# Two chained feed-forward layers: products in two 64-row halves of TensorE, two chunks at once

## The chip, the core and the metric

The kernel runs on one core of one Trainium2 chip. The metric is the device time of one execution in microseconds. Three runs of the kernel before took 1233.02, 1232.05 and 1232.23 us; the median is 1232.23.

## What is computed

Input is x (2 x 4096 tokens of 192 numbers, float32) and weight_gen (8 heads x 7 taps per token). A short causal convolution with per-token softmax weights comes first, then two feed-forward layers without bias, 192 to 2048 to 192:

```
w = softmax(weight_gen, axis=-1)
attn[b, s, h, :] = sum over k of w[b, s, h, k] * x_padded[b, s + k, h, :]
h = attn @ w_in;   g = h * cos(h);            y = g @ w_out      # layer 0
h = y @ moe2_w_in; g = maximum(0.01 * h, h);  out = g @ moe2_w_out   # layer 1
```

Everything is float32. The kernel keeps that precision by splitting each operand into a high and a low part of a shorter float type (fp32r) and adding the products hi x hi, lo x hi and hi x lo.

## The kernel before

**Tiles.** The 8192 tokens are 16 blocks of 512. A block's x stands transposed: 128 of its 192 numbers on the partitions of tiles hi and lo, the remaining 64 on both halves of the partitions of rh and rl (`x_tiles`, L388). The 2048 hidden units are 16 chunks of 128 (NF), so there are 2 layers x 16 blocks x 16 chunks = 512 chunks.

**One chunk** (`chunk`, L698). `hidden` (L708) forms h for 128 hidden units and 512 tokens in one bank of PSUM with five matmuls of 128 rows and 512 columns; the last two take the 64 remaining rows with their high weights on one half of the partitions and their low weights on the other:

```
terms = [(ihi, hi), (ilo, hi), (ihi, lo), (ir, rh), (ir, rl)]
for i, (w, v) in enumerate(terms):
    nc.tensor.matmul(h(), w[:, c], v(), start=i == 0, stop=i == len(terms) - 1)
```

Then comes the activation. In layer 0 (L743 to L753): ScalarE (or VectorE) rounds h / 2 pi to whole turns (L724), VectorE takes the angle (L731), ScalarE the sine (L736), VectorE multiplies by h (L741), ScalarE copies the high part (L262, a helper's line) and GpSimd subtracts to get the low part (L267). In layer 1 (L755 to L758): ScalarE's leaky ReLU, a copy of the high part, and VectorE's subtraction. `project_hi` (L767) and `project_lo` (L772) add the chunk's share of the second product with five more matmuls into two accumulators of the block, am (128 outputs) and ar (the other 64, high and low weights on different output partitions).

**Blocks.** `attention` (L395) makes a block's convolution on VectorE by token rows, and TensorE transposes it with six matmuls of 128 columns in two pieces (`turn`, `turn_rest`, L483 and L484); the first two blocks sum their seven taps on TensorE itself (`attention_summed`, L487, with L510). `turned` and `place` (L522, L543) split into high and low; ScalarE and VectorE copy the 64 remaining rows to the other half of the partitions (L552, L553). At a block's end `take` (L807) reads the accumulators; after layer 0 it makes the x tiles of layer 1, after layer 1 TensorE transposes back (L846, L847) and SyncE's queue stores (L853).

**Weights.** `weights` (L559) decodes 64-bit weights into high and low parts for 8 groups (2 layers x 4) of four chunks, in the first 200 us or so. ScalarE, VectorE and GpSimd share the work; four small DMAs a group (L666) move the remaining rows of w_in to their half of the partitions.

**Order.** Two streams of (layer, block) go side by side (L270 to L273), in the middle one with layer 0 and one with layer 1; the loop at L287 takes a chunk from each in turn (seq). Each operation is put into a plan with a due place in that order, a cost for each engine that may do it, and its buffers (`Plan.op`, L66); `Plan.emit` (L89) then goes through its own clock and issues, engine by engine, what can start first, near ties by due place. Each engine runs what it got strictly in that order. PSUM's eight banks are split: four shared by h and transposes, four accumulators (L242, L243). Rings hold 5 tiles g, 4 hi and 4 lo (L704 to L706). At the start TensorE is kept running by transposes of a constant (`keep_going`, L861).

## Time and profile before

| | |
|---|---|
| runs | 1233.02, 1232.05, 1232.23 us |
| span of the profiled execution, first to last instruction | 1230.4 us |
| granted TensorE clock, mean | 0.997 |
| TensorE busy (matmuls) | 1212.0 us, 98% |
| TensorE busy (weight loads, beside matmuls) | 998.8 us, 81% |
| VectorE, ScalarE, GpSimd busy | 891.2, 848.6, 449.1 us |
| DMA moved | 39.51 MB, mean 32 GB/s |

The profiled execution's own time is not listed beside its span; the median of the runs is 1.8 us above the span. Engines in rows: PE is TensorE's matmuls, PEld its weight loads, DVE is VectorE, ACT ScalarE, POOL GpSimd, SP SyncE; a small q behind a name means the engine's queue issuing DMAs. In a row, "out<-in" names tiles, "128x512" is partitions by elements, "x256" a count; after a bar come busy microseconds in all and mean nanoseconds of one, and then idle time ahead of it with what ended that. Matmuls are pipelined, so their lengths overlap: the distance from start to start is what one costs in a dense stretch.

### The profile page before, as it was taken

Reading aid. Unit: us, or ns where it says so; the run is one execution under the profiler, and the core shown is the slowest. Engines: PE = TensorE matmul, PEld = TensorE weight load, DVE = VectorE, ACT = ScalarE, POOL = GpSimd, SP = SyncE. Lnnn points to the kernel's source line nnn. Section 1 sums busy time; section 2 is a strip of 40 time slices with the busy share of each in tenths; the row PEclk is TensorE's granted clock in tenths of the full one; section 3 lists DMA queues with packets and bytes.
Section 4 is the critical chain, followed back from the end, with each engine's and each line's share of the span. In section 5 each row is a group of like instructions: output and inputs, shape, how many; then the busy total and the mean of one; then the engine's idle time right before and its main releaser. Section 6 shows DMA issues by size and latency. Waiting matters only on the chain.

```text
span 1230.4 us, 15323 instructions
## 1 busy us (share of the span) xinstructions
PE 1212.0 (98%) x5464; PEld 998.8 (81%) x5464; DVE 891.2 (72%) x1359; ACT 848.6 (69%) x1545; POOL 449.1 (36%) x340
## 2 busy tenths in 40 slices
PE   7999999999999999999999999999999999999998
PEld 6787877888888888888888888888888888888886
DVE  7988898988776777668577776767768586655433
ACT  5899767787766777676576767757666676655654
POOL 4878724663332423323232332323323333322000
PEclk9999999999999999999999999999999999999999
DMA  7344210200001010100101001010100100000000
GB/s 206 98 125 127 84 46 1 78 1 1 1 18 43 1 46 1 46 1 1 46 1 60 1 10 36 1 45 1 46 1 1 46 1 14 1 1 14 1 14 26
DMA packets 15469, 39.51 MB, mean 32 GB/s; under 512 B 1828, under 2 KB 8482, under 8 KB 15392
## 3 DMA queue, kind: packets, MB, share of 16 engines
q1 hardware_dynamic: 15392, 38.53, 9.8%
q8 instruction: 43, 0.70, 0.2%
q14 instruction: 34, 0.28, 0.1%
HBM read 30.13 MB, written 6.29 MB: 30 GB/s over the span
## 4 chain that ended last, share of the span: by engine, by line
PE 91%; DVE 4%; ACT 2%; DMA 1%; issue 1%; POOL 0%; SPq 0%; POOLq 0%; DVEq 0%; ACTq 0%
PE h L712 44%; PE acc0m L768 5%; PE acc1r L770 4%; PE acc0m L769 4%; PE acc0r L770 4%; PE acc0r L773 4%; PE acc1m L774 4%; PE acc1r L773 4%; PE acc0m L774 4%; PE acc1m L768 4%; PE acc1m L769 4%; DMA w00out<-in_moe_w_out 1%; DVE pr L436 1%; PE pm L839 1%; PE tm L476 0%
## 5 line engine op out<-in xcount | busy, mean ns | idle before, releaser
L267 POOL TENSOR_TENSOR lo<-g,hi 128x512 fp32r<-128x512 f32 x240 | 338.1, 1410 | 606.5 <-ACT hi L262 517.1
L731 DVE SCALAR_TENSOR_TENSOR g<-g,h 128x512 f32<-128x512 int32 x256 | 174.8, 685 | 158.7 <-ACT g L724 158.0
L267 DVE TENSOR_TENSOR lo<-h,hi 128x512 fp32r<-128x512 f32 x272 | 186.5, 688 | 93.5 <-ACT hi L262 91.8
L724 ACT ACTIVATE g<-h 128x512 int32<-128x512 f32 x233 | 138.3, 595 | 133.5 <-PE h L712 132.3
L755 ACT ACTIVATE h<-h 128x512 f32<-128x512 f32 x256 | 148.9, 582 | 86.5 <-PE h L712 85.6
L736 ACT ACTIVATE g<-g 128x512 f32<-128x512 f32 x256 | 160.3, 629 | 57.0 <-DVE g L731 56.2
L741 DVE TENSOR_TENSOR g<-h,g 128x512 f32<-128x512 f32 x240 | 164.6, 687 | 35.5 <-ACT g L736 30.5
L262 ACT ACTIVATE hi<-g 128x512 fp32r<-128x512 f32 x238 | 149.3, 629 | 47.1 <-DVE g L741 45.8
L262 ACT ACTIVATE hi<-h 128x512 fp32r<-128x512 f32 x228 | 135.3, 594 | 9.8 <-DVE h L741 1.2
L768 PE MATMUL acc0m<-hi,ohi 128*128 128x512 f32 x256 | 101.9, 398 | 2.4 <-ACT hi L262 2.4
L712 PE MATMUL h<-x0hi,ihi 128*128 128x512 f32 x256 | 100.3, 392 | 1.9 <-DVE lo L267 0.8
L773 PE MATMUL acc0r<-lo,or 128*128 128x512 f32 x256 | 100.6, 393 | 1.3 <-POOL lo L267 1.2
L768 PE MATMUL acc1m<-hi,ohi 128*128 128x512 f32 x256 | 101.8, 398 | 0.0
L712 PE MATMUL h<-x1hi,ihi 128*128 128x512 f32 x256 | 100.9, 394 | 0.4 <-DVE lo L267 0.4
L770 PE MATMUL acc1r<-hi,or 128*128 128x512 f32 x256 | 99.9, 390 | 0.4 <-POOL or L267 0.4
L769 PE MATMUL acc0m<-hi,olo 128*128 128x512 f32 x256 | 100.0, 391 | 0.0
L770 PE MATMUL acc0r<-hi,or 128*128 128x512 f32 x256 | 100.0, 391 | 0.0
L774 PE MATMUL acc0m<-lo,ohi 128*128 128x512 f32 x256 | 99.8, 390 | 0.0
L769 PE MATMUL acc1m<-hi,olo 128*128 128x512 f32 x256 | 99.8, 390 | 0.0
L773 PE MATMUL acc1r<-lo,or 128*128 128x512 f32 x256 | 99.8, 390 | 0.0
L712 PE MATMUL h<-x1rh,r 128*128 128x512 f32 x256 | 99.8, 390 | 0.0
L712 PE MATMUL h<-x1lo,ihi 128*128 128x512 f32 x256 | 99.8, 390 | 0.0
(254 smaller groups left out, 2462.6 us busy)
## 6 DMA issues: line engine op xcount, KB each, us to landing
xt<-in_x SPq DMA_DIRECT2D x12, 960.0 KB, 5.0
out<-osb SPq DMA_DIRECT2D x16, 384.0 KB, 2.6
smw<-in_weight_gen SPq DMA_DIRECT2D x3, 448.0 KB
xt<-in_x SPq DMA_DIRECT2D x3, 384.0 KB, 6.9
xt<-in_x SPq DMA_DIRECT2D x2, 576.0 KB, 7.5
r<-whi SPq DMA_DIRECT2D x16, 64.0 KB, 2.0
r<-wlo SPq DMA_DIRECT2D x16, 64.0 KB, 2.0
w00out<-in_moe_w_out SPq DMA_DIRECT2D x2, 384.0 KB, 8.4
```

The costliest lines, as they stand in the source:

```text
L262: nc.scalar.activation(out=out, in_=in_, func=AF.Copy)
L267: eng[e].tensor_tensor(out=out, in0=a, in1=b.bitcast(F32), op=ALU.subtract)
L712: nc.tensor.matmul(h(), w[:, c], v(), start=i == 0, stop=i == len(terms) - 1)
L731: nc.vector.scalar_tensor_tensor(out=g(), in0=g().bitcast(I32), scalar=-2 * math.pi, in1=h(), op0=ALU.mult, op1=ALU.add)
L736: nc.scalar.activation(out=g(), in_=g(), func=AF.Sin, bias=math.pi / 2)
L741: nc.vector.tensor_tensor(out=h() if bank_low else g(), in0=h(), in1=g(), op=ALU.mult)
L755: op(pos + 0.6, {"ACT": 0.58}, lambda e: nc.scalar.activation(out=h(), in_=h(), func=AF.Prelu, alpha=0.01), [kh], [kg], [h])
L768: nc.tensor.matmul(am(), ohi[:, f % GF, :], ghi(), start=first, stop=False)
L769: nc.tensor.matmul(am(), olo[:, f % GF, :], ghi(), start=False, stop=False)
L770: nc.tensor.matmul(ar(), orr[:, f % GF, :], ghi(), start=first, stop=False)
L773: nc.tensor.matmul(ar(), orr[:, f % GF, :], glo(), start=False, stop=last)
L774: nc.tensor.matmul(am(), ohi[:, f % GF, :], glo(), start=False, stop=last)
```

## The change

- TensorE is used as two halves of 64 rows. A chunk of even number has its first product on the lower half of the partitions (0 to 63), one of odd number on the upper half; so two chunks of the same block go at once. The 192 rows are three parts of 64, with three kinds of product each: 9 half-products. In the second product, each half takes 64 of a chunk's 128 hidden units: 5 half-products a chunk on each side. A pair of chunks so has 19 steps on either side.
- For that, x lies in three tiles of high and low parts: xn, xs (xn with its partition halves exchanged, written by two DMAs, `crossed`) and xr (the remaining 64 rows on both halves, the second by DMA where copies by ScalarE and VectorE stood). Loads of w_in put the chunks' rows straight on their half; the whi and wlo tiles and their DMAs go.
- The order of steps is a list for each side, made ahead: one side forms h of pair p and then adds pair p - 2 to the accumulators, the other adds pair p - 3 and then forms h of p. Where a side is about to write an accumulator's bank that the other side wrote, a wait (a nop on TensorE's queue with a semaphore) is put in front, on a matmul at least four steps back (APART). The list is cut into pieces that the plan issues in order; all pieces have one order key.
- The streams: after the first two blocks, whole blocks follow one another, layer 0 and layer 1 in turn.
- All eight banks of PSUM are one pool, with at most six for h. g, hi and lo have four tiles each at first; once all weights are decoded, the space of the raw weights becomes four more of each.
- The six transposes of a block are issued together, at a planner's cost that has 0.43 us more. Preparing a block is due eight chunk places ahead, not two.

The core of the diff:

```diff
--- before.py
+++ after.py
-    GAP = 3
-    TURN = 8
+    TURN = 12
     STAGGER = 6
+    LAG = 2
+    APART = 4
+    SWITCH = 0.43
+    FEW = 4
+    HELD = 6
+    EASE = 8
+    SIDES = (slice(0, P // 2), slice(P // 2, P))
...
-    xts = ctx.enter_context(tc.tile_pool(name="xts", bufs=4))
+    xts = ctx.enter_context(tc.tile_pool(name="xts", bufs=3))
     work = ctx.enter_context(tc.tile_pool(name="work", bufs=1))
-    ps = ctx.enter_context(tc.tile_pool(name="ps", bufs=4, space=PSUM))
-    psa = ctx.enter_context(tc.tile_pool(name="psa", bufs=1, space=PSUM))
+    raws = tc.tile_pool(name="raws", bufs=1, side="right")
+    space, places = {"raws": raws.__enter__()}, {}
+    ps = ctx.enter_context(tc.tile_pool(name="ps", bufs=1, space=PSUM))
...
+    def kept(tag, line):
+
+        def make():
+            (_, i) = b.held[0]
+            if (tag, i) not in places:
+                pool = work if i < FEW else space["late"]
+                places[tag, i] = pool.tile([P, T], F32 if tag == "g" else F32R, tag=f"{tag}{i}", bufs=1, name=f"{tag}{i}")
+            return places[tag, i]
+
+        b = Buf(make, tag, FEW, line=line)
+        return b
+
...
     def bank(name, kind):
-        return Buf(lambda: ps.tile([P, T], F32, tag="ps", name=name), "ps", 4, [kind])
+
+        def make():
+            (_, i) = b.held[0]
+            if ("ps", i) not in places:
+                places["ps", i] = ps.tile([P, T], F32, tag=f"ps{i}", name=f"ps{i}")
+            return places["ps", i]
+
+        b = Buf(make, "ps", 8, [kind] if kind else [])
+        return b
...
+    late = [(0, 2), (0, 3)]
+    for b in range(2, NB - 2):
+        late += [(1, b), (0, b + 2)]
+    streams = [[(0, 0), (1, 0), *late, (1, NB - 2), (1, NB - 1)], [(0, 1), (1, 1)]]
...
+    OUT = [(j, i) for j in range(2) for i in range(3)] + [(j, i) for j in range(2) for i in (3, 4)]
+    PAIRS = len(seq) // 2
+    lists = [[], []]
+    for p in range(PAIRS + LAG + 1):
+        for side in range(2):
+            q = p - LAG - side
+            ins = [("in", p, i) for i in range(9)] if p < PAIRS else []
+            outs = [("out", q, i) for i in range(10)] if 0 <= q < PAIRS else []
+            lists[side] += outs + ins if side else ins + outs
+
+    def part(step):
+        kind, p, i = step
+        return (kind, p) if kind == "in" else (kind, p, i // 3 if i < 6 else 2)
+
+    def bank_of(step):
+        kind, p, i = step
+        return (*seq[2 * p][1:3], "r" if i > 5 else "m") if kind == "out" else None
+
+    steps, at, last, known, log = [], [0, 0], {}, -1, []
+    while at[0] < len(lists[0]) or at[1] < len(lists[1]):
+        now = [None, None]
+        for side in range(2):
+            if at[side] == len(lists[side]):
+                continue
+            step = kind, p, i = lists[side][at[side]]
+            if side and kind == "out" and i == 0 and at[0] < len(lists[0]) and lists[0].index(("out", p, 9)) >= at[0]:
+                continue
+            before = last.get((1 - side, bank_of(step))) if kind == "out" else None
+            wait = None
+            if before is not None and before[1] > known:
+                if before[0] > len(steps) - APART:
+                    continue
+                wait = max(n for t, n in log if t <= len(steps) - APART)
+                known = wait
+            log.append((len(steps), len(log)))
+            if kind == "out":
+                last[side, bank_of(step)] = log[-1]
+            now[side] = (step, wait)
+            at[side] += 1
+        steps.append(now)
...
+    def crossed(m, b, due):
+        xn, xs, xr = x_of[m, b]
+        for j in range(2):
+            to, of_ = SIDES[j], SIDES[1 - j]
+            op(due, {"SP": 0.8}, lambda e, to=to, of_=of_: nc.sync.dma_start(
+                out=xs()[to].bitcast(F32), in_=xn()[of_].bitcast(F32)), [("xhi", m, b), ("xlo", m, b)], [("xs", m, b, j)], [xn, xs])
...
-        op(last, {"PE": 0.44}, turn, [("xam", b, q) for q in kinds] + ["ident"], [("tm", b)], [xa, tm])
-        op(last + 0.1, {"PE": 0.22}, turn_rest, [("xbr", b, q) for q in kinds] + ["ident"], [("tr", b)], [xb, tr])
+        def both(e):
+            turn(e)
+            turn_rest(e)
+
+        op(last, {"PE": 0.66 + SWITCH}, both, [(k, b, q) for q in kinds for k in ("xam", "xbr")] + ["ident"],
+           [("tm", b), ("tr", b)], [xa, xb, tm, tr])
...
-            op(due, {"ACT": 0.39}, lambda e, p=p, c=c: copy(e, rh()[p, c], v()[p]), [key], [("rh", m, b, i)], [rh, src])
-            op(due + 0.2, {"DVE": 0.42 if m == 0 else (0.41,)}, lambda e, p=p, c=c: minus(e, rl()[p, c], v()[p], rh()[p, c]),
-               [key, ("rh", m, b, i)], [("rl", m, b, i)], [rh, rl, src])
-        for i, ((p, c), (p2, _)) in enumerate(zip(halves, reversed(halves))):
-            op(due + 0.4, {"ACT": 0.39}, lambda e, p=p, p2=p2, c=c: copy(e, rh()[p2, c], v()[p]), [key], [("rh", m, b, 2 + i)], [rh, src])
-            op(due + 0.6, {"DVE": (0.29,)}, lambda e, p=p, p2=p2, c=c: copy(e, rl()[p2, c], rl()[p, c].bitcast(F32)),
-               [("rl", m, b, i)], [("rl", m, b, 2 + i)], [rl])
+            op(due, {"ACT": 0.39}, lambda e, p=p, c=c: copy(e, xr()[p, 0, c], v()[p]), [key], [("rh", m, b, i)], [xr, src])
+            op(due + 0.2, {"DVE": 0.42 if m == 0 else (0.41,)}, lambda e, p=p, c=c: minus(e, xr()[p, 1, c], v()[p], xr()[p, 0, c]),
+               [key, ("rh", m, b, i)], [("rl", m, b, i)], [xr, src])
+            op(due + 0.5, {"SP": 0.4}, lambda e, p=p, p2=SIDES[1 - i], c=c: nc.sync.dma_start(
+                out=xr()[p2, :, c].bitcast(F32), in_=xr()[p, :, c].bitcast(F32)), [("rh", m, b, i), ("rl", m, b, i)], [("rx", m, b, i)], [xr])
...
-        h = bank(f"h{m}_{b}_{f}", ("hq", 3))
-        g = temp([P, T], "g", 5, f"g_{pos}", line=f"g{st}")
-        ghi = temp([P, T], "hi", 4, f"hi_{pos}", F32R, f"hi{st}")
-        glo = temp([P, T], "lo", 4, f"lo_{pos}", F32R, f"lo{st}")
-
-        def hidden(e):
-            c = slice((f % GF) * P, (f % GF + 1) * P)
-            terms = [(ihi, hi), (ilo, hi), (ihi, lo), (ir, rh), (ir, rl)]
-            for i, (w, v) in enumerate(terms):
-                nc.tensor.matmul(h(), w[:, c], v(), start=i == 0, stop=i == len(terms) - 1)
-
-        reads = [((n, "a"), "hi", 0), ((n, "a"), "lo", 0)]
-        reads += [((n, "r"), i, j) for i in ("hi", "lo") for j in range(2)]
-        reads += [("xhi", m, b), ("xlo", m, b)] + [(i, m, b, j) for i in ("rh", "rl") for j in range(4)]
+        h = bank(f"h{m}_{b}_{f}", ("hq", HELD))
+        g, ghi, glo = (kept(i, f"{i}{st}") for i in ("g", "hi", "lo"))
+        side = f % 2
+        rows, j = SIDES[side], f % GF // 2
+
+        def hidden(i):
+            x, d = [(xn, side), (xr, 2), (xs, 1 - side)][i // 3]
+            w, v = [(ihi, 0), (ilo, 0), (ihi, 1)][i % 3]
+            return nc.tensor.matmul(h(), w[rows, j, d], x()[rows, v], start=i == 0, stop=i == 8)
+
+        first, last = f < 2, f >= NF - 2
+        if f == 0:
+            acc_of[st] = [bank(f"acc{m}{i}_{b}", None) for i in "mr"]
+        am, ar = acc_of[st]
+
+        def project(to_side, i):
+            to, w, v = [(am, ohi, ghi), (am, olo, ghi), (am, ohi, glo), (ar, orr, ghi), (ar, orr, glo)][i]
+            r = SIDES[to_side]
+            return nc.tensor.matmul(
+                to(), w[r, f % GF, :], v()[r], start=f == 0 and to_side == 0 and i in (0, 3),
+                stop=f == NF - 1 and to_side == 1 and i in (2, 4),
+            )
...
+        def run(e):
+            for now in nows:
+                for side, x in enumerate(now):
+                    if not x:
+                        continue
+                    (kind, p, i), wait = x
+                    if wait is not None:
+                        q = nc.tensor.nop()
+                        tc.add_manual_dep(q.ins, ran[wait].ins.name, sync, reason="bank")
+                    if kind == "in":
+                        ran.append(made["in", 2 * p + side][0](i))
+                    else:
+                        ran.append(made["out", 2 * p + OUT[i][0]][0](side, OUT[i][1]))
+
+        op(due, {"PE": len(nows) * MM}, run, reads, writes, bufs)
```

## Rows read from the trace of the kernel before

**Rows 1.** The page: busy times, and the chain by engine and by line
```profile
PE 1212.0 (98%) x5464; PEld 998.8 (81%) x5464; DVE 891.2 (72%) x1359; ACT 848.6 (69%) x1545; POOL 449.1 (36%) x340
PE 91%; DVE 4%; ACT 2%; DMA 1%; issue 1%; POOL 0%; SPq 0%; POOLq 0%; DVEq 0%; ACTq 0%
```

**Rows 2.** Table by stage: start:end, length, busy us (instructions) of each engine
```profile
core 0: us, PE busy (x) PEld busy (x) DVE busy (x) ACT busy (x) POOL busy (x), PEclk, DMA share, GB/s
0.00:20.00 20.00, 15.43 (x102) 14.15 (x103) 13.96 (x24) 8.66 (x17) 7.91 (x16) 0.91 0.79 221
20.00:200.00 180.00, 171.36 (x771) 137.85 (x770) 162.41 (x232) 146.22 (x255) 114.68 (x92) 0.99 0.31 93
...
400.00:500.00 100.00, 100.00 (x448) 82.71 (x448) 76.43 (x117) 72.72 (x132) 34.55 (x24) 1.00 0.04 15
...
1215.00:1230.40 15.40, 10.67 (x52) 8.25 (x50) 4.17 (x7) 6.09 (x12) 0.00 (x0) 1.00 0.14 53
```

**Rows 3.** Timeline of TensorE, 399.8 to 411.6 us: start, length, engine, line, operation
```profile
399.81 0.39 PE L712 MATMUL h<-x0hi,ilo 128*128 128x512 f32 x1
399.81 0.19 PEld L712 LDWEIGHTS h<-x0lo,ihi 128*128 128x128 f32 x1
...
400.04 0.39 PE L712 MATMUL h<-x0lo,ihi 128*128 128x512 f32 x1
400.04 0.19 PEld L712 LDWEIGHTS h<-x0rh,r 128*128 128x128 f32 x1
...
411.60 0.39 PE L768 MATMUL acc1m<-hi,ohi 128*128 128x512 f32 x1
```

**Rows 4.** Groups by line: one of the twenty alike; busy us, mean ns
```profile
L712 PE MATMUL h<-x1rl,r 128*128 128x512 f32 x256 | 99.7, 390 | 0.0
```

**Rows 5.** Timeline of TensorE around transposes (groups of four and two)
```profile
8.43 0.60 PE L510 MATMUL tr<-ident,pr 128*64 128x128 f32 x4
...
10.62 0.60 PE L510 MATMUL tm<-ident,pr 128*128 128x128 f32 x4
...
1221.46 0.60 PE L839 MATMUL pm<-ident,om 128*128 128x128 f32 x4
...
1221.90 0.38 PE L843 MATMUL pr<-ident,s 128*128 128x128 f32 x2
...
1222.35 0.39 PE L769 MATMUL acc1m<-hi,olo 128*128 128x512 f32 x1
```

**Rows 6.** Timeline of TensorE around one early stall
```profile
52.74 0.40 PE L774 MATMUL acc0m<-lo,ohi 128*128 128x512 f32 x1
54.28 0.51 PE L768 MATMUL acc0m<-hi,ohi 128*128 128x512 f32 x1 [1.15 <-ACT hi L262]
54.62 0.40 PE L769 MATMUL acc0m<-hi,olo 128*128 128x512 f32 x1
```

**Rows 7.** Stage 60 to 92 us: its table, and its layer-0 angles by line
```profile
60.00:92.00 32.00, 32.00 (x143) 26.47 (x142) 28.68 (x46) 29.09 (x51) 23.89 (x21) 1.00 0.40 120
...
L731 DVE SCALAR_TENSOR_TENSOR g<-g,h 128x512 f32<-128x512 int32 x14 | 9.6, 682 | 2.2 <-ACT g L724 2.0
```

**Rows 8.** Groups by line: ScalarE's three passes of a layer-0 chunk
```profile
L736 ACT ACTIVATE g<-g 128x512 f32<-128x512 f32 x256 | 160.3, 629 | 57.0 <-DVE g L731 56.2
L262 ACT ACTIVATE hi<-g 128x512 fp32r<-128x512 f32 x238 | 149.3, 629 | 47.1 <-DVE g L741 45.8
...
L724 ACT ACTIVATE g<-h 128x512 int32<-128x512 f32 x233 | 138.3, 595 | 133.5 <-PE h L712 132.3
```

**Rows 9.** DMA issues (KB each, median us to landing), and TensorE's first hidden product
```profile
out<-osb SPq DMA_DIRECT2D x16, 384.0 KB, 2.6
...
r<-whi SPq DMA_DIRECT2D x16, 64.0 KB, 2.0
...
20.58 0.47 PE L712 MATMUL h<-x0hi,ihi 128*128 128x512 f32 x1
```

More of the change, by code (lines that the diff above doesn't have):

```diff
@@ L169, in emit @@
                 self.at = max(self.at, o.due)
+            for b in o.bufs:
+                b.end = max(b.end, o.end)
             o.fn(e)
@@ L606, in weights @@
                 k = n, i, pn
[L607 removed]
+                due = need[m, g * GF] + WDUE[i]
                 def size(e, raw=raw, t=t, c=c):
@@ new lines, in conv_attention_moe_moe, with more @@
+    gate = Buf(lambda: None, "raw", 3, [("raw", 3)] * 2 + [("wa", 2)] * 2)
+    def more(e):
+        raws.__exit__(None, None, None)
+        space["late"] = ctx.enter_context(tc.tile_pool(name="late", bufs=1, side="right", reuse_waits="tile"))
+        for tag in ("g", "hi", "lo"):
+            plan.slots[tag] += [(gate.end, FEW + i) for i in range(FEW)]
+    weighed = [k for k in plan.writers if isinstance(k, tuple) and len(k) == 3 and k[1] in ("hi", "lo")]
+    op(0, {"SP": 0.0}, more, weighed, ["late"], [gate])
@@ new lines, in conv_attention_moe_moe @@
+    built = 0
+    for key, nows in pieces:
+        dues = []
+        for side, at in enumerate(key):
+            if at:
+                dues.append(2 * at[1] + side + (0 if at[0] == "in" else 2 * LAG + 1 + 0.3 * at[2]))
+                while at[0] == "in" and built <= 2 * at[1] + 1:
+                    st, m, b, f = seq[built]
+                    if f == 0 and m == 0:
+                        attention(b, tops[b])
+                    chunk(built, *seq[built])
+                    built += 1
+        piece(key, nows, max(dues))
```

266 lines of the change are left out of this document (134 added, 132 removed).

## The prediction

> **What bounds the kernel now.** I read the page's busy times and its chain first. TensorE is busy 98% of the span and holds 91% of the chain of work that ended last [rows 1]: nearly all of the time is matmuls one behind another. The table by stage then shows where that isn't so [rows 2]: the first 20 us (TensorE busy 15.4), the 180 us after them (171.4, while VectorE is busy 162.4, or 90%), and the last 15.4 us (10.7). In a stage from the middle TensorE is never idle, VectorE is busy 76%, ScalarE 73% and GpSimd 35%.
>
> So the price of one matmul decides. In the timeline a matmul of 512 columns starts at 399.81 us and the 52nd after it at 411.60 [rows 3]: 11.79 / 52 = 0.2267 us from start to start, though each lasts 0.39, so neighbours overlap by 0.163. Its weight load of 0.19 us begins as the matmul ahead of it starts; nothing waits for loads. There are twenty groups of 256 such matmuls [rows 4], so 5120 x 0.2267 = 1160.7 us. The other 344 of TensorE's 5464 are transposes [rows 1]; twenty of them take 10.62 - 8.43 = 2.19 us [rows 5], 0.109 each, 37.6 in all. That leaves 1230.4 - 1160.7 - 37.6 = 32.1 us of start, early waits and tail. The runs' median, 1232.23, is 1.8 above the span, and I carry that over unchanged. A difference of 0.2%, 2.5 us, is about the least that can be told from none.
>
> **The change, part by part.** *Halves of 64 rows.* A chunk's hidden product takes 9 half-products (three 64-row parts of the 192 rows, times hi x hi, lo x hi, hi x lo) where 5 full ones, ten halves, ran before; the lo x lo product of the last 64 rows goes. The second product stays at 10 halves. Each half of TensorE thus has 9 + 10 = 19 matmuls per two chunks, against 20 full ones. Going through the list that the diff builds gives 4889 steps (256 x 19 = 4864, and 25 for the lag at both ends; 50 steps have one half idle). The trace has no two half matmuls side by side. Its bounds are far apart: 0.2267 us a step if the halves run together, 0.4533 if one after the other. I take 0.2267, because each half then sees in a step just what the array sees now, one load of 128 columns and 512 columns of data, and the paths that both halves share bear it by the nearest row: a load and a transpose together pass in 0.109 us [rows 5], two such pairs in 0.219, under 0.2267. Term: (4889 - 5120) x 0.2267 = **-52.4 us**.
>
> *The sequencer.* A step issues four instructions. Two per 0.109 us is a rate that was reached, so 19,456 loads and matmuls, 688 for transposes and 924 new waits take at most 21,068 x 0.0547 = 1152 us, against 1108.3 + 37.6 = 1146 of array time: from 0 to +6; I take 0, since that row is a bound and need not be the sequencer's own pace.
>
> *Changes between whole and half array.* Transposes still use 128 rows. Today a group of six between matmuls costs only itself: from its start at 1221.46 to the second matmul after it at 1222.35 there are 0.89 us [rows 5], and 6 x 0.109 + 0.2267 is 0.88. By that row the term is 0. The Trainium skill (TensorEngine Tiling, section Tiling Modes, Key Properties) says that a change of tiling mode, not merely of tile, drains TensorE; no run here shows it yet. A drain is priced by rows: the overlap of 0.163 is lost at each of the two changes, 0.33 a group, and if the next load can't start before it either, 0.188 more at each, 0.70. Thirty groups (14 of inputs, 16 of outputs, each now issued as one piece) and about seven meetings with the second block's summed transposes give 0 to 26; in the middle of the drained prices, 37 x 0.5 = **+18.5 us**. By the first row alone the forecast would be 18.5 lower.
>
> *Waits between the halves.* The list puts a wait into TensorE's queue 924 times, so that one half's writes to an accumulator's bank are done before the other half's begin. All later matmuls stand behind it. It waits for a matmul at least four steps back, 0.91 us earlier, that is done after 0.39 [rows 3]; 0.52 us are left, more than a load's 0.188. Below, 0; above, a queue run dry at each wait: after a stall the first two matmuls are 0.34 us apart (54.28 to 54.62 [rows 6]), 0.113 more than usual, 104 us in all. I take **0**, by the 0.52 us of cover.
>
> *Crossed copies by DMA.* Each block's x is written into the other 64 partitions by SyncE's queue: two DMAs of 256 KB, and one or two of the remainder. The ScalarE and VectorE copies that did the latter go, as do 32 weight DMAs. SyncE issues in order, so a crossed copy can stand behind an output store that waits for its tile. A 64 KB copy lands after 2.0 us, a 384 KB store after 2.6 [rows 9]; preparation is eight chunk places, some 17 us, ahead, so in the middle they cost 0. Without that cover a block would wait some 2.5 us. At the start there is none: first matmul at 20.58 us [rows 9], crossed x needed from its seventh step, so +2.0 - 1.4 = about **+1 us** (0 to 3).
>
> *Start-up.* From 20 to 200 us VectorE is at 90% and TensorE already waits. If VectorE can't be driven harder, the 4.5% are not gained there: 180 x 0.045 = 8.1 us; otherwise 0. The hi and lo tiles number four until the weights are done, and a pair now waits two pairs for its second product. I take **+6 us**, near the upper end.
>
> *Layers one at a time.* A layer-0 chunk needs three ScalarE passes [rows 8], 1.85 us; alone that is 3.71 of a pair's 19 x 0.2267 = 4.31 us (86%), plus block work. From 60 to 92 us today's kernel runs layer 0 only: 14 chunks, TensorE 32.0 of 32, ScalarE 91% and VectorE 90% busy [rows 7]. So 0; what the wait costs without this is a rival. PSUM's one pool: two accumulators and some three h banks of eight stay under the cap: 0.
>
> *Tail.* Its one-sided steps are in the 4889.
>
> Sum: -52.4 + 18.5 + 1 + 6 = -26.9, from 1232.2 to **1205 us**.
>
> **Rivals.** *Layer 0 bound by ScalarE* (chance 0.10). For: 86% and block work at once, where layers were mixed before. Against: rows 7. A wait of 0.15 us in each of 128 layer-0 pairs gives 19 us: 1224.
>
> *The 924 waits are paid* (0.13). If the sequencer doesn't run ahead of the array, a wait restarts it: at half of rows 6's 0.113 us, 52 us, so 1258, slower than before. It decides from 26.9 / 924 = 0.029 us a wait. For: issue has only 0.008 us of room per step by the bound above. Against: the 0.52 us of cover. The Trainium skill (TensorEngine Tiling, Gotcha 1: PSUM Pressure) says that row tiles can't be at one PSUM bank together, so the waits can't simply go; no run here shows that.
>
> *The halves overlap only in part* (0.11, "it doesn't do what it says"). It decides from 26.9 / 4889 = 0.0055 us, a step of 0.2322; at 0.240 it is 1205 + 65 = 1270, with no overlap at all over 2290. For: no row has two matmuls side by side. Against: two load pairs in 0.219. The Trainium skill (TensorE: Matmul & The Clock Gate, Part 3, Measured speedup vs the span model) has 3.07x for four row tiles; at that share of the ideal a step would be 0.295, an estimate, and the time 1539. No row here bears that out.
>
> **How the numbers follow.** The forecast has 0.66; its own range runs from 1180 (only the steps) to 1217 (drains at 0.70, start 3, start-up 8.1). Layer 0 reaches 1224, the waits reach 1258; 1180 to 1262 leaves out some 0.05 below and 0.12 above. Faster: 0.66, 0.07 of the layer-0 case and 0.02 of mild waits, 0.75. Same: 0.04, from the edges of those two. Slower: 0.10 of the waits and 0.11 of the overlap, 0.21.
>
> **What would show it.** Half matmuls of two partition halves at the same start, pairs 0.2267 us apart: right; 0.232 or more: wrong. A gap of 0.3 to 0.7 us in matmul starts around each transpose group: drains. Gaps at the bank waits, every fifth step or so, would show that rival; matmuls waiting for GpSimd or ScalarE in layer-0 blocks the other. Start-up: the two-hundredth microsecond reached with no more chunks than before. The forecast fails if the middle isn't 4 to 4.5% faster.

## The result, and the profile after

The changed kernel takes **1209.68 us** (median of 4 runs, 1209.06 to 1211.85) against 1232.37 for the kernel before, measured beside it: a ratio of 0.9817, 95% interval 0.9804 to 0.9831. That is 22.7 us or 1.8% less, where 27 less were forecast. Its profiled execution spans 1208.1 us, against 1230.4 before. In a few executions the granted clock was lower and the time much longer (1470.97 us at 0.75 in one of them); the times below leave these out, and two kernels whose profile fell in one are told by their times alone.

The page: busy times, the chain by engine, and three of its DMA issues (KB each, median us to landing).

```profile
PE 1182.8 (98%) x10072; PEld 1016.0 (84%) x10072; DVE 886.1 (73%) x1299; ACT 847.0 (70%) x1484; POOL 443.0 (37%) x331
...
PE 92%; DMA 2%; DVE 2%; POOL 1%; issue 1%; ACT 1%; SPq 0%; DVEq 0%; POOLq 0%; ACTq 0%
...
x0s<-x0n SPq DMA_DIRECT2D x32, 256.0 KB, 3.8
x1s<-x1n SPq DMA_DIRECT2D x32, 256.0 KB, 3.7
out<-osb SPq DMA_DIRECT2D x16, 384.0 KB, 2.8
```

TensorE still holds the chain; its instructions have nearly doubled, because each is half a matmul. Against [rows 1] the other engines have hardly changed. By that page alone one can't see where 22 us went. The table by stage shows it (columns as in [rows 2]):

```profile
20.00:200.00 180.00, 164.27 (x1297) 136.51 (x1297) 155.65 (x226) 133.60 (x230) 108.50 (x82) 0.94 0.35 97
...
400.00:500.00 100.00, 100.00 (x870) 86.23 (x868) 74.48 (x111) 72.33 (x128) 33.07 (x24) 1.00 0.16 46
...
400.00:1100.00 700.00, 700.00 (x6076) 604.17 (x6074) 513.49 (x750) 495.42 (x870) 226.86 (x164) 1.00 0.15 42
```

The last of these stages in the kernel before:

```profile
400.00:1100.00 700.00, 700.00 (x3138) 578.77 (x3138) 500.98 (x774) 477.70 (x878) 227.15 (x162) 1.00 0.05 18
```

From 400 to 1100 us TensorE is never idle, before and after. In the changed kernel it ran 6076 instructions there; four of them began before 400 us, and the timeline has 19 groups of six transposes, so 5958 half matmuls began there, or 2979 steps of two. From 20 to 200 us TensorE is busy 164.3 us, where it was 171.4 before [rows 2], and its clock averages 0.94 against 0.99.

Counting products of 512 columns by time, in chunks, gives the course (my count of matmuls begun, from the timeline of TensorE; a chunk is 10 matmuls before and 19 half matmuls after):

| begun by | before | after |
|---|---|---|
| 60 us | 11.0 | 9.9 |
| 100 us | 28.5 | 27.4 |
| 140 us | 44.7 | 39.9 |
| 200 us | 69.1 | 64.7 |
| 400 us | 155.2 | 154.1 |
| 1000 us | 414.7 | 422.5 |

The changed kernel falls 4.4 chunks behind by 200 us, and gains 12.2 chunks from there to 1000 us. From 400 to 1000 us it does 268.4 chunks where the kernel before does 259.5: 3.4% more.

The halves do run side by side. The timeline of TensorE in the middle (start, length, engine, line, operation):

```profile
600.14 0.39 PE L789 MATMUL ps<-x0r,ilo 64*128 64x512 f32 x1
600.16 0.39 PE L799 MATMUL ps<-lo,ohi 64*128 64x512 f32 x1
600.37 0.39 PE L789 MATMUL ps<-x0r,ihi 64*128 64x512 f32 x1
600.38 0.39 PE L799 MATMUL ps<-hi,or 64*128 64x512 f32 x1
...
424.37 0.39 PE L789 MATMUL ps<-x1s,ihi 64*128 64x512 f32 x1
424.38 0.39 PE L799 MATMUL ps<-hi,or 64*128 64x512 f32 x1
424.70 0.66 PE L561 MATMUL ps<-ident,xa 128*128 128x128 f32 x4
425.20 0.38 PE L566 MATMUL ps<-ident,xb 128*128 128x128 f32 x2
425.51 0.50 PE L799 MATMUL ps<-lo,or 64*128 64x512 f32 x1
425.51 0.50 PE L799 MATMUL ps<-hi,ohi 64*128 64x512 f32 x1
425.85 0.40 PE L789 MATMUL ps<-x1n,ihi 64*128 64x512 f32 x1
```

Lines 789 and 799 are the hidden and the second product, each on its half; they start 0.01 to 0.02 us apart, and the next pair 0.23 later. The lower rows are a visit of transposes: from the pair at 424.38 to the one at 425.85 pass 1.47 us, in which two steps (0.45) fit; so the visit costs 1.02. Six transposes are 0.66 of that [rows 5]; **0.36 us** is new, and it is the change from half array to whole and back.

With that the mean step from 400 to 1100 us is (700 - 19 x 1.02) / 2979 = **0.2285 us**. The mean of all distances under 0.26 us from one start to the next on the timeline there is the same 0.2285 (two starts on, for halves), and 0.2271 for the whole matmuls of the kernel before.

The five largest waits of TensorE before 200 us (in all us, times, longest); the answer for the time after 200 us has one row, 1.2 us in the tail:

```profile
PE ps L789 <- POOL ilo L299: 7.0, 3, 3.7
PE ps L599 <- DVE pr L594: 3.1, 2, 2.6
PE ps L799 <- POOL olo L299: 2.7, 1, 2.7
PE ps L789 <- DVE x0n L299: 2.5, 1, 2.5
PE ps L789 <- DMA x0s<-x0n: 1.8, 2, 1.3
```

All are waits for data still being made: low parts of weights (ilo, olo) by GpSimd, sums of taps (pr) and low parts of x (x0n) by VectorE, and at the very start the crossed copy of x.

### The profile page after: what moved, and what is told of

It is laid out like the page before. It is cut to its first block, busy times and chain, and to the rows that moved or that the text cites. A ratio compares the mean times of both kernels' runs of the same rounds, so it can differ in the third digit from the quotient of the medians.

```text
span 1208.1 us, 25074 instructions
## 1 busy us (share of the span) xinstructions
PE 1182.8 (98%) x10072; PEld 1016.0 (84%) x10072; DVE 886.1 (73%) x1299; ACT 847.0 (70%) x1484; POOL 443.0 (37%) x331
## 4 chain that ended last, share of the span: by engine, by line
PE 92%; DMA 2%; DVE 2%; POOL 1%; issue 1%; ACT 1%; SPq 0%; DVEq 0%; POOLq 0%; ACTq 0%
PE ps L799 46%; PE ps L789 44%; PE ps L908 1%; DMA w01in<-in_moe_w_in 1%; PE ps L561 1%; PE ps L599 1%; DMA x1r<-x1r 1%; DMA xt<-in_x 0%; POOL ilo L299 0%; DMA x0s<-x0n 0%; PE ps L912 0%; DVE lo L299 0%; PE ps L566 0%; DVE g L828 0%; POOL w12in L725 0%
## 5 line engine op out<-in xcount | busy, mean ns | idle before, releaser
L799 PE MATMUL ps<-hi,ohi 64*128 64x512 f32 x1024 | 403.5, 394 | 0.0
L799 PE MATMUL ps<-hi,olo 64*128 64x512 f32 x1024 | 398.9, 390 | 2.7 <-POOL olo L299 2.7
L799 PE MATMUL ps<-lo,or 64*128 64x512 f32 x1024 | 399.6, 390 | 0.0
L799 PE MATMUL ps<-lo,ohi 64*128 64x512 f32 x1024 | 399.0, 390 | 0.1
L799 PE MATMUL ps<-hi,or 64*128 64x512 f32 x1024 | 398.5, 389 | 0.2 <-POOL or L299 0.2
L299 DVE TENSOR_TENSOR lo<-ps,hi 128x512 fp32r<-128x512 f32 x272 | 186.9, 690 | 162.9 <-ACT hi L294 156.8
L789 PE MATMUL ps<-x1n,ihi 64*128 64x512 f32 x512 | 199.6, 390 | 2.5 <-DVE x0n L299 2.5
L789 PE MATMUL ps<-x0s,ihi 64*128 64x512 f32 x512 | 198.6, 391 | 1.8 <-DMA x0s<-x0n 1.8
L789 PE MATMUL ps<-x1r,ihi 64*128 64x512 f32 x512 | 199.8, 390 | 0.5 <-DMA x1r<-x1r 0.5
L789 PE MATMUL ps<-x1s,ihi 64*128 64x512 f32 x512 | 199.2, 389 | 0.7 <-DMA x1s<-x1n 0.7
L789 PE MATMUL ps<-x0n,ihi 64*128 64x512 f32 x512 | 199.6, 394 | 0.2 <-DVE g L838 0.2
```

The lines of the kernel that those rows point to most:

```text
L299: eng[e].tensor_tensor(out=out, in0=a, in1=b.bitcast(F32), op=ALU.subtract)
L789: return nc.tensor.matmul(h(), w[rows, j, d], x()[rows, v], start=i == 0, stop=i == 8)
L799: return nc.tensor.matmul(to(), w[r, f % GF, :], v()[r], start=f == 0 and to_side == 0 and i in (0, 3), stop=f == NF - 1 and to_side == 1 ...
```

## The experiments

Each starts from the changed kernel unless it says otherwise. Times are medians, ratios are to the kernel before on the same chip.

### The new waits, each issued twice

```diff
-                        q = nc.tensor.nop()
-                        tc.add_manual_dep(q.ins, ran[wait].ins.name, sync, reason="bank")
+                        for _ in range(2):
+                            q = nc.tensor.nop()
+                            tc.add_manual_dep(q.ins, ran[wait].ins.name, sync, reason="bank")
```

> Each of the 924 bank waits on TensorE's queue is issued twice, nothing else changes. Theory (waits lie in the cover of four steps, TensorE's array sets the pace): no change, 1209 to 1211 us, and a step in the middle stays at 0.2285 us. Rival (the queue's issue is what stretches the step from 0.2267 to 0.2285, since a step issues four instructions): each further wait costs about one instruction of some 0.055 us, 924 x 0.055 = 51 us, so about 1260.

Measured: 1209.95 us, ratio 0.9814 (0.9799 to 0.9829). The table by stage of this kernel:

```profile
400.00:1100.00 700.00, 700.00 (x6076) 604.20 (x6074) 513.35 (x750) 494.87 (x869) 226.58 (x164) 1.00 0.15 42
```

To the instruction, the number of the changed kernel. Issuing the waits twice costs nothing, so room in the issue of instructions doesn't set the step. A second wait behind the first says nothing of how long the first one holds; for that, no distance between steps of the changed kernel from 400 to 1100 us is above 0.24 us outside the visits of transposes, so no wait stops TensorE there.

### The visits of transposes, split in two

```diff
-        op(last, {"PE": 0.66 + SWITCH}, both, [(k, b, q) for q in kinds for k in ("xam", "xbr")] + ["ident"],
-           [("tm", b), ("tr", b)], [xa, xb, tm, tr])
+        op(last, {"PE": 0.44 + SWITCH}, turn, [("xam", b, q) for q in kinds] + ["ident"], [("tm", b)], [xa, tm])
+        op(last + 1.2, {"PE": 0.22 + SWITCH}, turn_rest, [("xbr", b, q) for q in kinds] + ["ident"], [("tr", b)], [xb, tr])
...
-        op(due, {"PE": 0.66 + SWITCH}, both, [("om", m, b), ("s", m, b, 0), ("s", m, b, 1)],
-           [("pm", b), ("pr", b)], [om, s, pm, pr])
+        op(due, {"PE": 0.44 + SWITCH}, main, [("om", m, b)], [("pm", b)], [om, pm])
+        op(due + 1.2, {"PE": 0.22 + SWITCH}, rest, [("s", m, b, 0), ("s", m, b, 1)], [("pr", b)], [s, pr])
```

> The six transposes of a block go in two pieces again (four, then two, with matmul steps between them), as in the kernel before: 30 more visits to the whole-array mode. Theory (a visit costs 1.016 us in the trace, of which 0.656 are the six transposes, so 0.36 for the two changes): 30 x 0.36 = +11 us, about 1220. Rival (the 0.36 belongs to the transposes waiting or to the restart of cold halves, not to the change of mode): within 2 us of 1210.

Measured: 1225.04 us, ratio 0.9943 (0.9925 to 0.996), 15.4 us above the changed kernel. A visit of two transposes, in the timeline of TensorE:

```profile
428.30 0.39 PE L789 MATMUL ps<-x1n,ihi 64*128 64x512 f32 x1
428.62 0.44 PE L566 MATMUL ps<-ident,xb 128*128 128x128 f32 x2
428.99 0.50 PE L799 MATMUL ps<-hi,ohi 64*128 64x512 f32 x1
429.00 0.49 PE L789 MATMUL ps<-x1r,ihi 64*128 64x512 f32 x1
429.33 0.39 PE L789 MATMUL ps<-x1r,ilo 64*128 64x512 f32 x1
```

From 428.29 (the mean of the two halves) to 429.33 are 1.04 us; less two steps 0.59, less two transposes (0.22) 0.37. The visits of four give 0.36 in the same way. So the price belongs to the two changes and not to what is done between them, and 30 more visits account for 11 of the 15.4 us. Two other things changed, too. The step rose to 0.2306 us (distances under 0.26 us, as above), which is some 9 us from the sixtieth chunk on and isn't explained. And the start got faster: sixty chunks are begun by 184.1 us, where the changed kernel needs 188.7. 11 + 9 - 4.6 is near the 15.4.

### The halves without the new order of blocks

```diff
-    late = [(0, 2), (0, 3)]
-    for b in range(2, NB - 2):
-        late += [(1, b), (0, b + 2)]
-    streams = [[(0, 0), (1, 0), *late, (1, NB - 2), (1, NB - 1)], [(0, 1), (1, 1)]]
+    streams = [
+        [(0, 0), (1, 0), (0, 2)] + [(0, b) for b in range(4, NB)] + [(1, NB - 2)],
+        [(0, 1), (1, 1), (0, 3)] + [(1, b) for b in range(2, NB - 2)] + [(1, NB - 1)],
+    ]
```

> The order of blocks goes back to that of before (two streams, in the middle one with layer 0 and one with layer 1, taken a pair of chunks at a time); the halves stay. The list still has 4889 steps, but 544 waits instead of 924, and the accumulators of two blocks hold four of the eight banks. Theory (one layer at a time was not what gained or cost time; the middle is bound by TensorE in both orders): the middle keeps its step of 0.228 us and the whole lies within 1% of 1210. Rival A (waits cost some 0.01 us each): 380 fewer give -4 us. Rival B (PSUM is what the order was chosen for): with four banks left for h and transposes TensorE waits for banks, more than 1225.

Measured: 1255.97 us, ratio 1.0186 (1.0171 to 1.0201): **slower than before**, by 23 us. Its stage in the middle, its waits, and one of them in the timeline:

```profile
400.00:1100.00 700.00, 679.63 (x5777) 611.25 (x5775) 498.32 (x726) 465.04 (x822) 219.35 (x160) 1.00 0.14 40
```

```profile
PE ps L789 <- DVE g L838: 12.8, 24, 0.6
PE ps L789 <- DMA x0r<-x0r: 10.1, 11, 1.6
```

```profile
701.42 0.39 PE L799 MATMUL ps<-lo,or 64*128 64x512 f32 x1
701.43 0.39 PE L799 MATMUL ps<-hi,ohi 64*128 64x512 f32 x1
702.41 0.50 PE L789 MATMUL ps<-x1n,ihi 64*128 64x512 f32 x1 [0.60 <-DVE g L838]
702.42 0.50 PE L799 MATMUL ps<-hi,olo 64*128 64x512 f32 x1
702.76 0.40 PE L789 MATMUL ps<-x1n,ilo 64*128 64x512 f32 x1
```

TensorE runs 5777 instructions in the 700 us, not 6076. The hidden product (line 789) waits for a bank that VectorE's last pass over it (line 838) still reads, or for the crossed remainder of x. The last rows show why a short wait is dear: line 799's next matmul has no releaser of its own in its row, but it stands behind the waiting one in the same queue, and both halves start again at 702.41. A wait of 0.60 us makes 0.98 from start to start, where 0.23 is usual, and the next step is 0.35 long. This order has 544 bank waits where the changed kernel has 924, and its distances under 0.26 us have a mean of 0.2298: fewer waits don't make the step shorter.

### The new order of blocks without the halves

The kernel before, with only the order changed: these lines stand in place of its two streams, and its two sets of accumulators take turns.

```diff
+    late = [(0, 2), (0, 3)]
+    for b in range(2, NB - 2):
+        late += [(1, b), (0, b + 2)]
+    late += [(1, NB - 2), (1, NB - 1)]
+    streams = [[(0, 0), (1, 0)], [(0, 1), (1, 1)]]
...
+    for n, (m, i) in enumerate(late):
+        begin[m, LINE[i]] = len(seq)
+        seq += [(n % 2, m, LINE[i], f) for f in range(NF)]
+        end[m, LINE[i]] = len(seq) - 1
```

> The kernel before, with full 128-row products, and of the change only its order of blocks: after the first four blocks one block at a time, layers in turn (its two accumulator sets are still used in turn). Theory (the order is no gain of its own, it only lets the halves pay): the middle of the kernel before has no idle TensorE and 5120 products at 0.2267 us, which no order can shorten, so 1232 us, within 1229 to 1236, and 448 of TensorE's instructions per 100 us in the middle as before. Rival A (the order is worth something by itself, and part of the 22.7 us belongs to it): 1226 or less. Rival B (a layer-0 block alone is bound by ScalarE or VectorE even at 20 products per two chunks): 1240 or more, with TensorE waiting for ScalarE or VectorE in layer-0 blocks.

Measured: 1235.43 us (11 runs), ratio 1.002 (1.0011 to 1.0029). Alone the order costs 2.5 us. So neither part is a gain by itself: the order +2.5, the halves +23, both together -22.7.

### Banks of the hidden products: four, not six

```diff
-    HELD = 6
+    HELD = 4
```

> At most four PSUM banks for h, not six; the pool stays at eight. Theory (with one layer at a time some three banks of h are in use, so that six is slack, and the order by two streams was slow because four accumulators and two transpose banks leave h only two): no change, 1208 to 1212. Rival (h needs more than four banks to bridge the two pairs of lag): TensorE waits for banks and the time rises by more than 10 us.

Measured: 1211.42 us, ratio 0.982 (0.9804 to 0.9837). In the new order the hidden products get by with four banks; a shortage of banks alone, at this number, isn't what makes the old order slow.

### Parts of an accumulator five steps apart, not four

```diff
-    APART = 4
+    APART = 5
```

> A half may write a bank only five steps after the other half wrote it, not four. The number of matmuls and loads stays 9728 each, the waits are 916, but the list has 5098 steps instead of 4889, 468 of them with one half idle instead of 50. Theory (a step is the unit of time: 0.2267 to 0.2285 us whether one half or both are at work): 209 x 0.228 = +48 us, about 1257. Rival (issue of instructions is the unit, some 0.057 us each): the number issued is the same, so no change, 1208 to 1212.

Measured: 1213.29 us, ratio 0.9842 (0.9826 to 0.9858): 3.6 us more, not 48. In the stage from 400 to 1100 us TensorE ran as much as in the changed kernel:

```profile
400.00:1100.00 700.00, 700.00 (x6072) 639.10 (x6070) 495.55 (x744) 500.37 (x873) 214.19 (x163) 1.00 0.16 43
```

The list has 5098 steps now, 468 of them with one half idle, and they aren't paid. A step of the list is no barrier: a half that has nothing in one step goes on with its next, and idle places of one half are made good by those of the other. What is paid is the number of matmuls on each half, 4864. The few microseconds more come at the end: the last product begins 3.0 us later than in the changed kernel, and only 0.9 at the third chunk from the end.

### Transposes on the halves too

```diff
-            turn(e)
-            turn_rest(e)
+            v = xb().rearrange("p j a r -> p j (a r)")
+            half_turns([(tm()[:, q * P : (q + 1) * P], xa()[:, q, :P]) for q in range(Q)],
+                       [(tr()[:, j * P : (j + 1) * P], v[:, j]) for j in range(2)])
...
+    def half_turns(pairs_a, pairs_b):
+
+        def one(pair, side):
+            to, of_ = pair
+            c = slice(side * HP, (side + 1) * HP)
+            return nc.tensor.transpose(to[:, c], of_[SIDES[side]], ident[SIDES[side], c])
+
+        for x, y in ((0, 1), (1, 0)):
+            for i, p in enumerate(pairs_a):
+                q = one(p, x)
+                if i < len(pairs_b):
+                    one(pairs_b[i], y)
+            if not x:
+                hold = nc.tensor.nop()
+                tc.add_manual_dep(hold.ins, q.ins.name, sync, reason="bank")
...
-            main(e)
-            rest(e)
+            half_turns([(pm()[:, q * P : (q + 1) * P], om()[:, q * P : (q + 1) * P]) for q in range(Q)],
+                       [(pr()[:, j * P : (j + 1) * P], s()[:, j * P : (j + 1) * P]) for j in range(2)])
```

> The thirty visits of six whole transposes become twelve transposes of 64 rows, six on each half, with one more wait in the middle so that the halves are not in one bank together; the transposes of the first two blocks stay whole. Theory (0.36 us of each visit is the change of mode, and halves run side by side): a visit falls from 1.02 us to 6 x 0.055 + 0.25 for the wait = 0.6, 30 x 0.4 = -12 us, about 1197. Rival A (the mode costs, but the halves' transposes do not overlap): 0.66 + 0.25 = 0.9, -3 us, about 1206. Rival B (issue binds: 24 instructions at 0.055 us): 1.3 us or more a visit, 1218 or more.

Measured: **1204.47 us** (1203.73 to 1205.59), ratio 0.9768 (0.9753 to 0.9782), faster than both. The same visit as above, in its timeline:

```profile
423.57 0.39 PE L808 MATMUL ps<-x1s,ihi 64*128 64x512 f32 x1
423.69 0.28 PE L648 MATMUL ps<-ident,xa 64*128 64x64 f32 x2
...
424.42 0.47 PE L818 MATMUL ps<-hi,ohi 64*128 64x512 f32 x1
424.62 0.39 PE L808 MATMUL ps<-x1n,ihi 64*128 64x512 f32 x1
424.74 0.39 PE L818 MATMUL ps<-hi,olo 64*128 64x512 f32 x1
```

Here the halves run 0.11 us apart. On the half whose matmul starts at 423.57 the second one after the visit starts at 424.74: 1.17 us, less two steps 0.71 (0.72 in the mean of the 19 visits from 400 to 1100 us), against 1.02. Thirty visits save 9.0 us by that; the median fell by 5.2 and the span by 5.8. The timeline places most of what is missing: sixty chunks are begun 0.8 us later than in the changed kernel, the last product begins 7.3 earlier, and the stretch behind it is 1.5 longer. A visit of 0.72 lies between the 0.6 of the theory and the 0.9 of the first rival, and the time is nearer the rival's.

### The start: what holds it

Five kernels tried to win back the 4.4 chunks.

Weights asked for sooner:

```diff
-    WDUE = {"in": -0.6, "out": 4.0}
+    WDUE = {"in": -4.0, "out": 1.0}
```

> The weights' due places move: w_in from 0.6 to 4 chunk places ahead of their first use, w_out from 4 behind to 1 behind. Theory (in the first 200 us TensorE waits 9.9 us for the weights' low parts from GpSimd because the plan ranks them too late, and its clock then falls to the lower level): the waits shrink and the time falls by 4 to 10 us, to 1200 to 1206. Rival (VectorE and GpSimd have no room there, as the prediction said): other work is pushed back instead, and the time stays within 1208 to 1214.

Measured: 1217.42 us (1209.46 to 1219.04, an unusual spread), ratio 0.985 (0.9815 to 0.9885). No gain; the waits go over to the tap sums, as this kernel's waits of TensorE show:

```profile
PE ps L599 <- DVE pr L594: 11.3, 3, 4.9
PE ps L789 <- DMA x1r<-x1r: 3.5, 1, 3.5
```

The second load of input weights held until the first crossed copies have landed:

```diff
-                        op(due - 6, {"SP": 0.65}, lambda e, raw=raw, j=j, side=side: load(raw, j, side), (), [("raw", n, i, j, side)], [raw])
+                        op(due - 6, {"SP": 0.65}, lambda e, raw=raw, j=j, side=side: load(raw, j, side),
+                           [("xs", 0, LINE[0], k) for k in range(2)] if (m, g) == (0, 1) else (), [("raw", n, i, j, side)], [raw])
...
+    attention(LINE[0], tops[LINE[0]])
...
-                    if f == 0 and m == 0:
+                    if f == 0 and m == 0 and b != LINE[0]:
```

> The load of the second group of w_in waits until the first block's crossed copies have landed (the kernel before held that load back too, for its remainder copies; the change lets it go at once). Theory (the first crossed copies take 3.9 us because weight loads fill the DMA engines, which stops TensorE for some 3 us at 21 to 25 us and lets its clock fall until 31): they land in 2 to 2.5 us, TensorE's start gains 2 to 5 us, 1205 to 1208. Rival (the second group is then itself late): TensorE waits longer for its low part near 51 us, and the time is 1209 to 1214.

Measured: 1211.76 us, ratio 0.9825 (0.9809 to 0.9842). No gain. That the copies are slow by themselves is shown by the changed kernel's page: 3.7 to 3.8 us is their median over the whole run.

The first wait filled, so that TensorE doesn't stand still: 60 half transposes, whose results nothing reads, between the sixth and the seventh step.

```diff
...
+                    if kind == "in" and (p, side, i) == (0, 0, 6):
+                        for n in range(60):
+                            c = slice(n % 8 * P // 2, (n % 8 + 1) * P // 2)
+                            nc.tensor.transpose(spare()[:, c], ident[SIDES[0]], ident[SIDES[0], : P // 2])
```

> Sixty transposes of a constant, on one half, fill the wait for the first crossed copies (21 to 25 us); the output of these goes nowhere. Theory (the idle stretch is what lets the granted clock fall to the lower level from 24 to 31 us, and that costs some 3 us): the clock stays at the upper level there, the first two pairs' products end about 3 us sooner, and the time is 1206 to 1208. Rival (what follows is bound by the second block's taps on VectorE and by the weights, so the 3 us are given back at the next wait): 1209 to 1211, with the clock up all the same.

Measured: 1210.85 us, ratio 0.9823 (0.981 to 0.9837). In the changed kernel the wait at 23 us is followed by steps 0.43 us apart, because the granted clock is 0.50, the lower of its two levels (1.2 GHz, not 2.4), from 24 to 30 us. This is the stage in the changed kernel, and a part of it:

```profile
20.00:32.00 12.00, 10.16 (x52) 7.04 (x51) 10.88 (x18) 7.27 (x13) 8.03 (x8) 0.72 0.32 85
...
26.00:28.00 2.00, 2.00 (x12) 1.56 (x10) 2.00 (x4) 1.47 (x5) 1.51 (x3) 0.50 0.00 0
```

and this with the wait filled:

```profile
20.00:32.00 12.00, 11.55 (x125) 10.37 (x124) 11.08 (x18) 7.27 (x14) 7.90 (x8) 1.00 0.34 92
```

The clock stays at its upper level and the first two pairs end 1.3 us sooner, and by 200 us no more chunks are begun (64.4). What is won is given back at later waits.

More tiles for the second product. First rings of six for g, hi and lo, with two sets of x instead of three to make room:

```diff
-    FEW = 4
+    FEW = 6
...
-    xts = ctx.enter_context(tc.tile_pool(name="xts", bufs=3))
+    xts = ctx.enter_context(tc.tile_pool(name="xts", bufs=2))
...
```

> The rings of g, hi and lo begin with six tiles each instead of four, and grow to eight as before; the room comes from two sets of x tiles instead of three. Theory (four tiles don't span the two pairs of lag, so that in the first 200 us each stall of one engine is passed on to TensorE at once, and its clock falls): by 200 us TensorE is one to three chunks further than the 64.5 of the changed kernel, the time 1203 to 1207. Rival (the start is bound by when the weights' low parts come, whatever the rings): 64 to 65 chunks by 200 us, 1208 to 1212, or more if two sets of x are too few.

Measured: 1299.68 us, ratio 1.054 (1.0525 to 1.0554). Then five tiles of hi and lo only, paid for with one buffer of the remainder of x (the core of it):

```diff
-    FEW = 4
+    MOST_OF = {"g": 4, "hi": 5, "lo": 5}
...
-                pool = work if i < FEW else space["late"]
+                pool = work if i < MOST_OF[tag] else space["late"]
...
-            Buf(lambda i=i: xts.tile([P, 2, T], F32R, tag=f"x{i}", name=f"x{m}{i}{b}"), f"x{i}", 3)
+            Buf(lambda i=i: xts.tile([P, 2, T], F32R, tag=f"x{i}", bufs=2 if i == "r" else 3, name=f"x{m}{i}{b}"), f"x{i}", 2 if i == "r" else 3)
...
```

> The changed kernel with five tiles each of hi and lo until the weights are done, not four (the third buffer of the input's remainder goes to make room, the two main parts keep three). Theory (the rings of four hold the start-up back, because a pair waits two pairs for its second product): a part of the 10 us that start-up loses to the kernel before comes back, 1203 to 1207 us, and 66 or more chunks done by 200 us (64.5 in the changed kernel, 69.1 before). Rival (what holds the start-up is when weights and taps are ready, on VectorE and GpSimd): 1208 to 1212, 64 to 65 chunks by 200 us, and the same waits for the second weights' parts. If two buffers of the remainder are too few, matmuls wait for the crossed copies of the remainder in the middle and the time is above 1215.

Measured: 1266.87 us, ratio 1.0272 (1.0257 to 1.0286). Both are slow in the middle, for want of x; these are the later kernel's two largest waits, the first all after 200 us, the second all before:

```profile
PE ps L789 <- DMA x0r<-x0r: 35.7, 12, 3.0
PE ps L789 <- POOL ilo L299: 13.9, 4, 5.6
```

Three buffers are needed, then, of the remainder of x at least: the kernel with two of all three tiles, too, waits for the remainder (62.3 us in 13 waits, by far its largest). For the start the second row counts. By 60 us this kernel has begun 11.3 chunks, as many as the kernel with doubled waits, which has four tiles (11.3); the 9.9 of the changed kernel come of a later start that is made up soon after (20 chunks are begun by 83.6 us there, and by 83.0 with doubled waits). By 140 us it has 39.0 against 44.7 before, by 200 us 65.8 against 69.1, where the changed kernel has 64.7. So the fifth tile wins back about a quarter of the 4.4 chunks in this execution, though its wait for ilo is 13.9 us and not 7.0 (11.7 in the kernel with parts five steps apart, which has four tiles). The last low part of weights that GpSimd makes, in the timeline of the kernel before:

```profile
154.46 1.31 POOL L267 TENSOR_TENSOR olo<-w13out,ohi 128x512 fp32r<-128x512 f32 x1
```

and of the changed one:

```profile
161.02 1.90 POOL L299 TENSOR_TENSOR olo<-w13out,ohi 128x512 fp32r<-128x512 f32 x1
```

It is done at 162.9 us, 7 later than before, and in the kernel with five tiles at 163.7. My reading is that from about 100 us the start goes at the pace at which VectorE, GpSimd and the loads make weights and tap sums: sooner weights delay tap sums, and more room for TensorE's work wins little while the weights are late. This is argued and not shown. The split visits show that another order of the same work at the start can win 4.6 us there; which order of those engines' queues would win the rest is open.

## Why the prediction was right, point by point

The forecast, 1205 us with faster at 0.75, had the sign and the mechanism, and was 4.7 us too low. That it came so near is in part luck: the steps gave 8.8 us less than forecast and the start cost 2.1 more, and the changes of mode cost 6.3 less. In the spans, its terms against what they measured:

| term | predicted | measured | from |
|---|---|---|---|
| steps | -52.4 | -43.6 | 4889 x 0.2285 - 1160.7 |
| changes of mode | +18.5 | +12.2 | 34 visits x 0.36 |
| start and crossed copies | +7 | +9.1 | the rest: 1208.1 - 1117.1 - 37.6 - 12.2 = 41.2, against 32.1 |
| sum | -26.9 | -22.3 | spans, 1230.4 to 1208.1 |

**The steps.** Right in kind: the halves run side by side, and a step is nearly what one full matmul was. The step that failed by a little is "I take 0.2267": it is 0.2285, 0.8% longer, which is 8.8 us. The kernel before too is at 0.2271 over the same stage, so about a fifth of this is that I took a clean stretch's figure [rows 3] for the average. What lengthens the step further isn't settled. It isn't issue (doubled waits changed nothing) or the number of waits (the old order has fewer and a longer step), and it isn't the visits, which are taken out. It isn't the copies by DMA in the main: cut into slices of 2 us, the middle has 0.2284 in the 228 slices in which DMA moves 1 GB/s or less, and 0.2293 in the 55 with more than 150 (my count). The count 4889 was near for another reason than given: the list's steps are not the unit, the 4864 matmuls of each half are.

**The overlap rival** (a step of 0.232 or more) is decided by the 0.2285, under its turning point of 0.2322. The Trainium skill (TensorE: Matmul & The Clock Gate, Part 3, Measured speedup vs the span model) has 3.07x for four row tiles, 77% of the ideal; two row tiles here reach 0.4533 / 0.2285 = 1.98x, so that share doesn't carry over.

**The sequencer and the 924 waits**: 0 and 0, right. The rival at 1258 us fell: the measured time is below it, TensorE has no gap in the middle, and doubled waits cost nothing.

**Changes of mode.** Here two readings stood against each other: [rows 5] gave 0, and the drain gave 0.33 to 0.70 a visit. 0.36 was measured, alike for two, four and six transposes; the row of before had no change of mode in it, so it said nothing on this. The Trainium skill (TensorEngine Tiling, section Tiling Modes, Key Properties) states that such a change drains TensorE; the trace agrees, at 0.36 us a visit. The step that was mis-sized is "in the middle of the drained prices, 0.5": the price is near the low one, the overlap of 0.163 lost twice. And 34 visits are paid, not 37: four at the start and thirty.

**Crossed copies.** "+1 us" was made with a landing of 2.0 us, that of a 64 KB copy [rows 9]. The copies of 256 KB land in 3.7 to 3.8, longer than a 384 KB store (2.8). The nearer row by size would have been the store. At the start the seventh step is complete at 24.62 us on its second half, where the sixth is at 21.20: some 3 us late, not 1. The kernels with the load held and with the wait filled won nothing back in the end (2.1 and 1.2 us more than the changed kernel).

**Start-up.** "+6, near the upper end" with 8.1 as the bound. The measured 9.1 us lies above the bound; 4.4 chunks behind at 200 us, times 19 / 2 x 0.2285, are 9.6, so the two counts agree. The reasoning (VectorE can't be driven harder) would give a stage as fast as before, not a slower one; and VectorE is less busy in it, 155.7 us against 162.4. What it left out is that the weights come later: the waits for their low parts, 7.0 and 2.7 us, have next to no like in the kernel before (0.4 us, for a part of or), and several stops are followed by a stretch at a lower clock. The stage from 100 to 140 us, before and after:

```profile
100.00:140.00 40.00, 38.09 (x164) 30.00 (x163) 34.58 (x49) 36.67 (x63) 32.48 (x26) 1.00 0.48 146
```

```profile
100.00:140.00 40.00, 32.12 (x243) 25.25 (x241) 33.84 (x45) 26.66 (x46) 28.41 (x20) 0.91 0.59 156
```

Of the two causes named, the four tiles of hi and lo are a small part (about a quarter, in one execution of a kernel that changes something else, too).

**One layer at a time** was costed at 0, with "the halves" as a gain that stands by itself. For the change as a whole the 0 is about right (the order alone is +2.5). But the text took the order for an addition, and it is a condition: with the old order the halves lose 23 us. With blocks of both layers at once TensorE waits for crossed remainders and for banks, and a wait of one half stops the other. The rows prove the waits; that the number of accumulators is their first cause is only argued. That order and halves came in one change, so that the 0 held, is luck. The ScalarE rival for layer 0 fell: no wait of TensorE between 200 us and the tail.

**The last sign**, "the forecast fails if the middle isn't 4 to 4.5% faster", is not met as it stands: the middle does 3.4% more. The sign was set by the steps alone, and most of the forecast's own 18.5 us of mode changes lie in the middle. With the visits taken out, a chunk takes 19 / 2 x 0.2285 us where it took 10 x 0.2271, 4.4% less.

## What to carry to other kernels

When an array is split into halves that feed from one queue, price the step by the matmuls of each half, and then look for every wait of either half: the halves share the queue, so it stops both. Price each visit in another tiling mode at the overlap lost at both edges, whatever is done in between, and ask whether the visit can be made in the same mode. A part of a change that is worth nothing alone may be what the rest depends on, so test each part with and without the others.

## What was not expected of the hardware

- A change from 64-row to 128-row use of TensorE and back costs 0.36 us, the same for two, four and six transposes between.
- Two 64-row matmuls of 512 columns pass together in 0.2285 us, against 0.2271 for one of 128 rows over the same stretch.
- Copies of 256 KB from SBUF to SBUF land in 3.7 to 3.8 us, later than a store of 384 KB in 2.8.
- Transposes of float32 in 64-row halves run in both halves between the matmuls: the first starts 0.12 us after the last matmul (423.69, 423.57), where a whole one starts 0.32 after it (424.70, 424.38). A visit of twelve costs 0.72 us, against 1.02 for six whole ones.
